# Moving a quarter of a modulation vector from one-column matmuls to VectorE: eight k-tiles added in two chains, then four one-column sums on PE

## The chip, the cores and the metric

One core of one Trainium2 chip. The metric is the device time of one execution in microseconds (us); lower is better. Before the change it is 831.41 us (median of 3 runs, 831.29 to 831.42).

PE is TensorE, PEld its weight loads, DVE is VectorE, ACT is ScalarE, SP issues the DMAs. All times inside a trace count from the start of its span.

## The reference, cut to what matters

```python
mod = (_silu(c) @ w_mod)            # six vectors of 1024: sa, ca, ga, sb, cb, gb
h = _layernorm(x) * (1 + ca) + sa   # x: 2048 x 1024
qkv = h @ wqkv                      # then linear attention, wo, and a SwiGLU FFN
```

Only the scale vector `ca` is touched, and of it only columns 768 to 1023. It is needed very early: the first q products multiply `h`.

## The kernel before

`h` is kept transposed in `HT`, so the scale is one value per partition for each k-tile `dt` (128 of the 1024 columns that the products sum over). The two vectors are made by one-column matmuls with the weights stationary, eight k-tiles per 128 columns, all in one corner of bank 0 of PSUM (where PE leaves its sums; the second index of the tile `PS` is the bank):

```python
def mod_sc(w, c0, ms):
    for m in ms:
        for kt in range(NDT):                       # NDT = 8
            P.pe("matmul", out=PS[:, 0, c0 + m:c0 + m + 1], lhsT=w[:, kt, m * 128:(m + 1) * 128],
                 rhs=SILUC[:, kt:kt + 1], start=mod_first[0], stop=(kt == NDT - 1), skip_group_check=True)
            mod_first[0] = False

def fin_ca(m, n):                                   # VectorE reads bank 0
    P.dve("tensor_scalar", out=MODCOL[:, 0, m:m + n], in0=PS[:, 0, 8 + m:8 + m + n], scalar1=1.0, ...)
```

The first q phase threads these between the q products (`q_part`, 512 columns wide, one bank per `nt`):

```python
# ... q products of k-tiles 0 and 1, scale columns 0 to 3 ...
mod_sc(WCA, 8, range(4, 8))            # 32 products
fin_ca(4, 4)
for dt in (4, 5):
    h0_scale_only(dt)                  # VectorE
for nt in range(7):
    q_part(nt, qb[nt], (2, 3))
act_stats(4)
for nt in range(7):
    if nt == 4:
        mod_sc(WSA, 0, range(6, 8))    # shift columns 6, 7: bank 0 again
        fin_sa(6, 2)
        for dt in (6, 7):
            h0_scale(dt)               # needs scale and shift columns 6, 7
    q_part(nt, qb[nt], (4, 5))
mod_sc(WSA, 0, range(4, 6))
fin_sa(4, 2, True)
for nt in range(7):
    if nt == 2:
        bias_mm((4, 5))                # one-column products, bank 0
    q_part(nt, qb[nt], (6,))
# ... k-tile 7, shift columns 0 to 3, then one long run of products ...
```

The helper that records the operations keeps, for each PSUM bank, the last operation of each engine, and makes an access wait for the other engines' last access of the whole bank, whatever the columns:

```python
for bank in banks:
    st = self.excl.get(bank)
    if st:
        for e2, d in st.items():
            if e2 != eng:
                deps_add(d)
    self.excl[bank] = {eng: op}
```

While the first chunk's q and k run on PE, the next chunk of `h` is transposed by DMA, four tiles one after the other, and then modulated (scaled and shifted) on VectorE, one k-tile at a time; the first k group of chunk 1 takes these k-tiles in order:

```python
def th_dma(st):
    xbar(HT[:, buf, :, j * 128:(j + 1) * 128], XRES[:, st, :])      # DMA transpose; st = 4 to 7 here
for dt in range(NDT):
    add(kside, 1, lambda dt=dt: th_mod(1, dt))                      # VectorE, 128 x 512 each
```

And at the start PE runs warm-up products on constant data: `warm(13, bank=3)`, later `warm(5, bank=3)`.

Of the kernel before, what the change touches and what calls it, by code (L numbers as in the profile page):

```python
# [6 lines left out]
BF16 = mybir.dt.bfloat16  # L7
U8 = mybir.dt.uint8
ACT = mybir.ActivationFunctionType
ALU = mybir.AluOpType  # L10
# [252 lines left out]
def bass_adaLN_cond__linear_attn_block__swiglu_ffn__prompt_kernel(  # L263
# [17 lines left out]
    NDT = D // 128  # L281
# [4 lines left out]
    with ExitStack() as es:  # L286
# [6 lines left out]
        def T(name, off, shape, dt):  # L293
            n = 1
            for s_ in shape[1:]:
                n *= s_
            assert off % 32 == 0 and off + n * mybir.dt.size(dt) <= ARENA, (name, off, shape)
            return nc.alloc_sbuf_tensor_at(name, shape, dt, offset=base + off)
# [4 lines left out]
        WCA = T("wca", 32 * KB, [128, NDT, D], BF16)  # L303
        WSA = T("wsa", 48 * KB, [128, NDT, D], BF16)
        AT = T("at", 72 * KB, [128, NFT, 512], BF16)
        SM = 64 * KB
# [7 lines left out]
        MODCOL = T("modcol", SM + 1120, [128, 4, NDT], FP32)  # L314
# [13 lines left out]
        ZCOL = T("zcol", SM + 2304, [128, NHG], FP32)  # L328
        RED = T("red", SM + 2336, [128, NDT], FP32)
        MASK4 = T("mask4", SM + 2368, [128, 4], BF16)  # L330
        BIASQ = T("biasq", SM + 2784, [128, NDT], FP32)
        SUMXH = T("sumxh", SM + 2816, [128, NST, 2], FP32)
        NMR = T("nmr", SM + 2944, [128, NST], FP32)
# [5 lines left out]
        HT = T("ht", 120 * KB, [128, 2, NDT, 512], BF16)  # L339
# [7 lines left out]
        ACC = T("acc", 192 * KB, [128, D], FP32)  # L347
        MHL = T("mhl", 196 * KB, [128, 2, D], BF16)
# [7 lines left out]
        SILUF = T("siluf", SM + 7744, [128, NDT], FP32)  # L356
# [22 lines left out]
        PS = nc.alloc_psum_tensor("ps", [128, 8, 512], FP32)  # L379
# [15 lines left out]
        P = _Prog()  # L395
# [47 lines left out]
        P.dve("memset", ap=MASK[:], constant=0.0)  # L443
        for h in range(4):
            P.dve("memset", ap=MASK[32 * h:32 * h + 32, 32 * h:32 * h + 32], constant=1.0)
        P.dve("memset", ap=MASK4[:], constant=0.0)
        for h in range(4):
            P.dve("memset", ap=MASK4[32 * h:32 * h + 32, h:h + 1], constant=1.0)
        P.dve("memset", ap=ZSEL[:], constant=0.0)
# [54 lines left out]
        def mod_sc(w, c0, ms):  # L504
            for m in ms:
                for kt in range(NDT):
# [4 lines that stand above are left out]
        def fin_ca(m, n):  # L511
            P.dve("tensor_scalar", out=MODCOL[:, 0, m:m + n], in0=PS[:, 0, 8 + m:8 + m + n], scalar1=1.0, scalar2=None,
                  op0=ALU.add)

        def fin_sa(m, n, cast=False):
            if cast:
                P.dve("tensor_copy", out=MODTMP[:, m:m + n], in_=PS[:, 0, m:m + n])
            P.dve("tensor_copy", out=MODCOL[:, 1, m:m + n], in_=PS[:, 0, m:m + n])

        def h0_scale_only(dt):  # L520
            P.dve("tensor_scalar", out=HT[:, 0, dt, :], in0=HT[:, 1, dt, :], scalar1=MODCOL[:, 0, dt:dt + 1],
                  scalar2=None, op0=ALU.mult)

        def h0_shift(dt):
            P.dve("tensor_scalar", out=HT[:, 0, dt, :], in0=HT[:, 0, dt, :], scalar1=MODCOL[:, 1, dt:dt + 1],
                  scalar2=None, op0=ALU.add)
# [7 lines left out]
        def bias_fin():  # L534
            P.dve("tensor_copy", out=BIASQ[:], in_=PS[:, 0, 16:24])

# [3 lines left out]
        def h0_first(dt, eng):  # L540
            if eng == "act":
                P.act("activation", out=HT[:, 0, dt, :], in_=t_view(dt), func=ACT.Copy, scale=MODCOL[:, 0, dt:dt + 1])
            else:
                P.dve("tensor_scalar", out=HT[:, 0, dt, :], in0=t_view(dt), scalar1=MODCOL[:, 0, dt:dt + 1],
                      scalar2=None, op0=ALU.mult)
# [8 lines left out]
        def h0_scale(dt):  # L554
            P.dve("tensor_scalar", out=HT[:, 0, dt, :], in0=HT[:, 1, dt, :], scalar1=MODCOL[:, 0, dt:dt + 1],
                  scalar2=MODCOL[:, 1, dt:dt + 1], op0=ALU.mult, op1=ALU.add)
# [17 lines left out]
        def act_stats(st, c0=0, mid=None):  # L574
            n = (D - c0) // 512
            junk0 = HT[:, 1, 0:2, :] if st < 8 else JUNK1
            for fn_, sc_, acc_ in ((ACT.Identity, 1.0 / D, SUMX), (ACT.Square, D ** -0.5, SUMSQ)):
                P.act("activation", out=junk0[:, 0:n, :], in_=XRES[:, st, c0:D].rearrange("p (a b) -> p a b", a=n),
                      func=fn_, scale=sc_, accum_out=acc_[:, st:st + 1])
                if mid is not None:  # L580
                    mid()
                    mid = None
# [90 lines left out]
        def q_part(nt, bank, dts):  # L673
            for dt in dts:
                P.pe("matmul", out=PS[:, bank, :], lhsT=WQK[:, dt, nt * 128:(nt + 1) * 128],
                     rhs=HT[:, 0, dt, :], start=(dt == 0), stop=(dt == 7))
# [56 lines left out]
        def q_phase_chunk0(side):  # L733
            qb = [1, 2, 3, 4, 6, 7, 5]
            for nt in range(4):
                q_part(nt, qb[nt], (0,))
            mod_sc(WCA, 8, range(2, 4))
            fin_ca(2, 2)
            for dt in (2, 3):
                h0_first(dt, "dve")  # L740
            for nts, dts in (((4, 5), (0,)), (range(6), (1,)), ((6,), (0, 1))):
                for nt in nts:
                    q_part(nt, qb[nt], dts)
            mod_sc(WCA, 8, range(4, 8))
            fin_ca(4, 4)
            for dt in (4, 5):
                h0_scale_only(dt)
            for nt in range(7):
                q_part(nt, qb[nt], (2, 3))
            act_stats(4)  # L750
            for nt in range(7):
                if nt == 4:
                    mod_sc(WSA, 0, range(6, 8))
                    fin_sa(6, 2)
                    for dt in (6, 7):
                        h0_scale(dt)
# [5 lines that stand above are left out]
                    bias_mm((4, 5))  # L762
                q_part(nt, qb[nt], (6,))
            for nt in range(7):
                if nt == 1:
                    mod_sc(WSA, 0, range(4))
                    fin_sa(0, 4, True)
                    ln_ops[1][0]()
                    ln_ops[1][1]()
                if nt == 4:  # L770
                    bias_mm(range(4))
                    bias_fin()
                q_part(nt, qb[nt], (7,))
            ln_ops[1][2]()
            ln1_rstd1(5)
            for f in act_mv_ops(4):
                f()
            neg_rstd(4)
            q_phi = lambda nt: phi_evac(qb[nt] if nt < 7 else 0, PQT[:, nt, 0:512], bias=BIASQ[:, nt:nt + 1])
            for i, dt in enumerate((4, 5, 0, 1, 2, 3, 6, 7)):  # L780
                P.pe("matmul", out=PS[:, 0, :], lhsT=WQK[:, dt, 896:1024], rhs=HT[:, 0, dt, :], start=(i == 0),
                     stop=(i == 7))
            for dt in (4, 5):
                h0_shift(dt)
            ln1_xn(5)
            th_dma(5)
            for dt in range(4):
                h0_shift(dt)
            ln1_xn(4)
            th_dma(4)  # L790
            for nt in range(8):
                q_phi(nt)
                for f in side.get(nt, []):
                    f()
            qk_ctr[0] = 0
# [40 lines left out]
        def z_cols():  # L836
# [4 lines left out]
                  in0=ZHL[:, 0, 0:NDT].unsqueeze(2).to_broadcast([128, NHG, 4]),  # L841
                  in1=MASK4[:].unsqueeze(1).to_broadcast([128, NHG, 4]), op=ALU.mult)

# [249 lines left out]
        for ch in range(NCH):  # L1093
            nxt = ch + 1 if ch + 1 < NCH else None
            for ft in range(NFT):
# [4 lines left out]
                for dt in range(NDT):  # L1100
                    P.pe("matmul", out=PS[:, gbank, :], lhsT=GUG[slot][:, dt, ftl * 128:(ftl + 1) * 128],
                         rhs=H2T[:, dt, :], start=(dt == 0), stop=(dt == NDT - 1))
                for dt in range(NDT):
                    P.pe("matmul", out=PS[:, ubank, :], lhsT=GUU[slot][:, dt, ftl * 128:(ftl + 1) * 128],
                         rhs=H2T[:, dt, :], start=(dt == 0), stop=(dt == NDT - 1))
# [4 lines left out]
                if ch == 0 and ft % 2 == 0 and ft < 14:  # L1110
                    i = ft // 2
# [11 lines left out]
                if nxt is None and ft in (8, 12):  # L1123
# [3 lines left out]
                          in1=GB_B[:, 896:1024].unsqueeze(1).to_broadcast([128, f1 - f0, 128]), op=ALU.mult)  # L1127
# [5 lines left out]
            for j in range(4):  # L1133
# [3 lines left out]
                if not last:  # L1137
                    for ft in range(NFT):
                        for nh in range(2):
                            P.pe("matmul", out=PS[:, bb + nh, :], lhsT=AT[:, ft, j * 128:(j + 1) * 128],  # L1140
                                 rhs=WD(ft)[:, nh * 512:nh * 512 + 512], start=(ft == 0), stop=(ft == NFT - 1))
                for nh in range(2):
                    i = nh
                    parts = [(0, 384, bb + 1), (384, 512, 4)] if last and nh == 1 else [(0, 512, bb + nh)]
                    for (c0, c1, pb) in parts:
                        if last:
                            for ft in range(NFT):
                                P.pe("matmul", out=PS[:, pb, c0:c1], lhsT=AT[:, ft, j * 128:(j + 1) * 128],
                                     rhs=WDG[:, ft, :] if c0 > 0 else WD(ft)[:, nh * 512 + c0:nh * 512 + c1],
                                     start=(ft == 0), stop=(ft == NFT - 1))  # L1150
# [46 lines left out]
```

## Time and profile before

| what | value | view |
|---|---|---|
| time, median | 831.41 us | runs |
| span in the profile | 829.3 us | page |
| PE busy | 99% | page |
| PE without a break | 12.29 to 827.1 us | chain in order of time |
| 16, 32 one-column products hold PE for | 0.40, 0.80 us | timeline of PE |

PE is the limit.

The end of the chain that ended last, in order of time (start, length, what):

```profile
12.29 814.80 PE ps L176 x4016
...
827.11 0.29 DVE xres L176
```

From 12.29 us on, for 814.80 us, nothing but PE is on it; only the last residual addition follows. A change after that is worth what it does to PE's own sequence.

The timeline of PE in the first q phase (start us, length us, engine, line, operation, out<-in, shape, count). The modelled end of a group of matmuls overlaps the next, so times are taken from start to start; a few matmul records are missing from some traces, as in a count of 21 for 22:

```profile
13.56 2.32 PE L176 MATMUL ps<-ht,wqk 128*128 128x512 bf16 x10
15.71 0.94 PE L176 MATMUL ps<-siluc,wca 128*128 128x1 bf16 x32
16.51 4.91 PE L176 MATMUL ps<-ht,wqk 128*128 128x512 bf16 x22
21.26 0.54 PE L176 MATMUL ps<-siluc,wsa 128*128 128x1 bf16 x16
21.66 1.46 PE L176 MATMUL ps<-ht,wqk 128*128 128x512 bf16 x6
...
27.84 1.46 PE L176 MATMUL ps<-ht,wqk 128*128 128x512 bf16 x6
```

32 scale products start at 15.71 and the next q product at 16.51: 25 ns each. 22 q products take 16.51 to 21.26: 0.216 us each. 16 shift products take 21.26 to 21.66. From the ten q products at 13.56 to the long run at 27.84 the stage takes 14.28 us. This interval leaves out when PE could start.

Two lines of VectorE's timeline in the same stretch, in brackets the idle time before them and what ended it. It has time to spare:

```profile
16.75 0.16 DVE L176 TENSOR_SCALAR modcol<-ps 128x4 f32<-128x4 f32 x1 [1.89 <-PE ps L176]
...
21.84 0.16 DVE L176 COPY modcol<-ps 128x2 f32<-128x2 f32 x1 [4.27 <-PE ps L176]
```

### The profile page before, as it was taken

The numbers are of one execution on the slowest core, as the hardware profiler recorded it, in microseconds if no ns is written. First come the engines' busy times: TensorE is split into PE (matmuls) and PEld (weight loads), VectorE is DVE, ScalarE is ACT, GpSimd is POOL, SyncE is SP. The second block draws the span as 40 slices with busy tenths as digits, with TensorE's granted clock in tenths as the row PEclk, the third lists the DMA queues.
The fourth block names the chain that finished last, engine by engine and source line by source line (L and its number), as shares of the span: only waits on it lengthen the run. The fifth ranks groups of instructions, "written<-read, shape, count | busy, mean of one in ns | idle before, by whom it ended". The sixth has DMA issues, their size and how long they took to land.

```text
span 829.3 us, 10017 instructions
## 1 busy us (share of the span) xinstructions
PE 823.3 (99%) x4083; PEld 378.8 (46%) x4083; DVE 312.9 (38%) x666; ACT 196.3 (24%) x335; POOL 40.5 (5%) x58
## 2 busy tenths in 40 slices
PE   8999999999999999999999999999999999999998
PEld 4544444454444444444444444444444444444444
DVE  5797986756955521121221111122111211221111
ACT  3658641323232111111111111111110111111011
POOL 1010000000130000030000003000000300000000
DMA  9969655938297986700455571045557004553000
GB/s 320 284 152 229 150 162 172 197 107 304 57 256 226 262 256 184 194 25 13 123 152 153 152 188 34 13 124 154 152 153 193 27 13 124 151 154 91 0 26 26
DMA packets 199246, 119.29 MB, mean 144 GB/s; under 512 B 57880, under 2 KB 182944, under 8 KB 199200
## 3 DMA queue, kind: packets, MB, share of 16 engines
q1 hardware_dynamic: 199184, 118.65, 53.0%
q8 instruction: 32, 0.52, 0.3%
q14 instruction: 14, 0.11, 0.0%
q10 hardware_dynamic: 16, 0.00, 0.0%
HBM read 100.67 MB, written 4.33 MB: 127 GB/s over the span
## 4 chain that ended last, share of the span: by engine, by line
PE 98%; DMA 1%; DVE 0%; ACT 0%; SPq 0%; POOL 0%; issue 0%
PE ps L176 98%; DMA xres<-in_A_x_dram 1%; ACT ht L176 0%; DVE xres L176 0%; SPq L176 0%; POOL rstd L176 0%; DVE stats L176 0%; DVE mv L176 0%; DVE ve L176 0%
## 5 line engine op out<-in xcount | busy, mean ns | idle before, releaser
L176 PE MATMUL ps<-h2t,gug 128*128 128x512 bf16 x896 | 211.7, 379 | 0.0
L176 PE MATMUL ps<-h2t,guu 128*128 128x512 bf16 x896 | 211.7, 379 | 0.0
L176 DVE TENSOR_TENSOR at<-sg,ps 128x512 bf16<-128x512 bf16 x112 | 77.0, 687 | 282.8 <-PE ps L176 281.2
L176 ACT ACTIVATE sg<-ps 128x512 bf16<-128x512 f32 x112 | 66.9, 597 | 309.7 <-PE ps L176 309.7
L176 PEld LDWEIGHTS ps<-h2t,guu 128*128 128x128 bf16 x896 | 87.7, 98 | 105.7
L176 PEld LDWEIGHTS ps<-h2t,gug 128*128 128x128 bf16 x896 | 87.6, 98 | 105.5
L176 PE MATMUL ps<-wd_a,at 128*128 128x512 bf16 (+1 forms) x512 | 112.4, 377 | 0.0
L176 PE MATMUL ps<-ht,wqk 128*128 128x512 bf16 x512 | 111.8, 379 | 0.1
L176 PE MATMUL ps<-wd_b,at 128*128 128x512 bf16 (+1 forms) x384 | 85.0, 377 | 0.0
L176 PEld LDWEIGHTS ps<-wd_a,at 128*128 128x128 bf16 x512 | 50.1, 98 | 59.7
L176 DVE TENSOR_TENSOR ut<-att,gb_b 128x512 bf16<-128x512 bf16 (+1 forms) x32 | 14.1, 441 | 167.0 <-ACT att L176 167.0
L176 PEld LDWEIGHTS ps<-ht,wqk 128*128 128x128 bf16 x512 | 49.4, 98 | 58.7 <-issue 0.2
L176 ACT ACTIVATE att<-ps 128x512 bf16<-128x512 f32 (+1 forms) x32 | 17.4, 591 | 182.1 <-PE ps L176 182.1
L176 PEld LDWEIGHTS ps<-wd_b,at 128*128 128x128 bf16 x384 | 37.6, 98 | 44.7
L176 PE MATMUL ps<-pk,xres 128*128 128x512 bf16 x256 | 56.5, 379 | 0.0
L176 PE MATMUL ps<-mw,pqt 128*128 128x512 bf16 x256 | 56.3, 379 | 0.0
L176 POOL TENSOR_SCALAR h2t<-h2t,modcol 128x512 bf16<-128x512 bf16 x32 | 26.3, 836 | 383.4 <-DMA h2t<-xn 383.4
L176 ACT ACTIVATE e<-ps 128x512 bf16<-128x512 f32 x56 | 33.1, 603 | 31.8 <-PE ps L176 21.3
L176 PEld LDWEIGHTS ps<-mw,pqt 128*128 128x128 bf16 x256 | 24.8, 98 | 30.2 <-DVE xres L176 0.4
L176 PEld LDWEIGHTS ps<-pk,xres 128*128 128x128 bf16 x256 | 24.8, 98 | 30.0 <-issue 0.4
L176 ACT ACTIVATE junk<-xres 128x1024 bf16<-128x1024 bf16 x24 | 25.4, 1058 | 35.1 <-DVE xres L176 34.9
L176 DVE SCALAR_TENSOR_TENSOR xres<-ps,xres 128x512 bf16<-128x512 f32 x32 | 21.4, 688 | 12.3 <-PE ps L176 11.5
(106 smaller groups left out, 345.1 us busy)
## 6 DMA issues: line engine op xcount, KB each, us to landing
gug<-in_B_w_gate_dram SPq DMA_DIRECT2D x56, 512.0 KB, 3.9
guu<-in_B_w_up_dram SPq DMA_DIRECT2D x56, 512.0 KB, 5.2
xres<-in_A_x_dram SPq DMA_DIRECT2D x20, 256.0 KB, 8.0
rb<-recip_den SPq DMA_DIRECT2D x8, 512.0 KB, 11.5
stgx<-in_w_mod_dram SPq DMA_DIRECT2D x2, 2048.0 KB, 7.8
wd_a<-in_B_w_down_dram SPq DMA_DIRECT2D x4, 1024.0 KB, 8.0
out_dram<-xres SPq DMA_DIRECT2D x31, 128.0 KB, 1.7
xres<-in_A_x_dram SPq DMA_DIRECT2D x3, 1024.0 KB, 14.2
```

The lines of the kernel that those rows point to most:

```text
L176: return getattr(e, method)(**kw)
```

## The change

The 16 products of scale columns 6 and 7 (768 to 1023) leave PE. VectorE multiplies and adds the eight k-tiles of these 256 columns in two alternating chains of fp32, adds the two, and splits the result into a bf16 part and a bf16 remainder. PE sums over the partitions: two 128-column pieces, times two parts, against a column of ones. The two scalings of k-tiles 4 and 5 go from VectorE to ACT, to make room. The intent is to free PE of 12 products net, with engines that idle.

```diff
+        P.dve("memset", ap=ONESC[:], constant=1.0)
...
+        def part_macc_ops(w, c0, n):
+            acc = [ACC[:, i * n:(i + 1) * n] for i in range(2)]
+            for kt in range(NDT):
+                a, src, sc = acc[kt % 2], w[:, kt, c0:c0 + n], SILUF[:, kt:kt + 1]
+                # ... kt < 2: tensor_scalar mult; else scalar_tensor_tensor mult, add into a
+            # ... acc[0] += acc[1]; MHL[0] = bf16(acc[0]); MHL[1] = acc[0] - MHL[0]
+        def part_sum(c0, ms):
+            for m in ms:
+                for i in range(2):
+                    P.pe("matmul", out=PS[:, 0, c0 + m:c0 + m + 1], lhsT=MHL[:, i, m * 128:(m + 1) * 128],
+                         rhs=ONESC[:], start=False, stop=(i == 1), skip_group_check=True)
...
         def h0_scale_only(dt):
-            P.dve("tensor_scalar", ...)
+            P.act("activation", ..., func=ACT.Copy, scale=MODCOL[:, 0, dt:dt + 1])
...
-            mod_sc(WCA, 8, range(4, 8))
-            fin_ca(4, 4)
+            mod_sc(WCA, 8, range(4, 6))
+            mops = part_macc_ops(WCA, 768, 256)
+            for f in mops[:4]:
+                f()
+            fin_ca(4, 2)
+            for f in mops[4:]:
+                f()
...
                 if nt == 4:
+                    part_sum(8, (6, 7))
+                    fin_ca(6, 2)
                     mod_sc(WSA, 0, range(6, 8))
```

(Cuts are marked with dots.)

More of the change, by code (lines that the diff above doesn't have):

```diff
@@ L330, in bass_adaLN_cond__linear_attn_block__swiglu_ffn__prompt_kernel @@
         MASK4 = T("mask4", SM + 2368, [128, 4], BF16)
+        ONESC = T("onesc", SM + 2400, [128, 1], BF16)
         BIASQ = T("biasq", SM + 2784, [128, NDT], FP32)
@@ L518, in fin_sa @@
             P.dve("tensor_copy", out=MODCOL[:, 1, m:m + n], in_=PS[:, 0, m:m + n])
+        def part_macc_ops(w, c0, n):
+            acc = [ACC[:, i * n:(i + 1) * n] for i in range(2)]
+            ops = []
+            for kt in range(NDT):
+                a, src, sc = acc[kt % 2], w[:, kt, c0:c0 + n], SILUF[:, kt:kt + 1]
+                if kt < 2:
+                    ops.append(lambda a=a, src=src, sc=sc: P.dve("tensor_scalar", out=a, in0=src, scalar1=sc,
+                                                                 scalar2=None, op0=ALU.mult))
+                else:
+                    ops.append(lambda a=a, src=src, sc=sc: P.dve("scalar_tensor_tensor", out=a, in0=src, scalar=sc,
+                                                                 in1=a, op0=ALU.mult, op1=ALU.add))
+            ops.append(lambda: P.dve("tensor_tensor", out=acc[0], in0=acc[0], in1=acc[1], op=ALU.add))
+            ops.append(lambda: P.dve("tensor_copy", out=MHL[:, 0, c0:c0 + n], in_=acc[0]))
+            ops.append(lambda: P.dve("tensor_tensor", out=MHL[:, 1, c0:c0 + n], in0=acc[0], in1=MHL[:, 0, c0:c0 + n],
+                                     op=ALU.subtract))
+            return ops
+        def part_sum(c0, ms):
[3 more added lines that the diff above has]
+                         rhs=ONESC[:], start=False, stop=(i == 1), skip_group_check=True)
         def h0_scale_only(dt):
-            P.dve("tensor_scalar", out=HT[:, 0, dt, :], in0=HT[:, 1, dt, :], scalar1=MODCOL[:, 0, dt:dt + 1],
-                  scalar2=None, op0=ALU.mult)
+            P.act("activation", out=HT[:, 0, dt, :], in_=HT[:, 1, dt, :], func=ACT.Copy,
+                  scale=MODCOL[:, 0, dt:dt + 1])
         def h0_shift(dt):
```

## The prediction

> **What bounds the kernel now.** TensorE. The page gives PE 99% busy; the chain that ended last, in order of time, is PE without a break from 12.29 us to 827.1 us, and the table of waits has no PE wait after that start. So the change is worth only what it takes from or adds to PE's own sequence between 12 and 28 us. DVE and ACT have room: in the timeline DVE idles from 14.9 to 16.75 and from 17.6 to 21.84, ACT from 14.8 to 25.9.
>
> **What leaves PE.** 16 of the 32 one-column products with the scale weights. In the timeline 16 such products hold back the next q matmul by 0.40 us (21.26 to 21.66), 32 by 0.80 (15.71 to 16.51): 25 ns each, as the Trainium skill states for small matmuls ("TensorE: Matmul & The Clock Gate", Back-to-back issue gap). Four new hi/lo products cost 0.10. Net -0.30 us.
>
> **What DVE gets.** Estimated from the trace's longer versions (128x1024: multiply-add 1279 ns, first multiply 750, copy 684, subtract 1226; multiply-add at 512 columns 688): at 256 columns two multiplies of 0.3 us, six multiply-adds of 0.4, add 0.4, copy 0.3, subtract 0.4: about 4 us. They start at about 14.9 (weights landed at about 13.95), let the read of columns 4-5 in at 16.4, and end at about 19.2; PE wants the sums at about 20.7. The two scalings moved to ACT (0.6 us each) end near 18; PE needs them at 19.2. None of this is critical.
>
> **What it adds as a wait.** The helper serializes whole PSUM banks between engines. The sum products write bank 0, VectorE then reads two columns of bank 0, and the next PE work is the shift products, also in bank 0. PE must wait for that read, with no q matmul between. The same handoff stands in the trace: after the products at 22.95, two q matmuls (0.43 us) precede the bias products, and these still start 0.10 us later than 22.95 + 0.40 + 0.43. VectorE does one read more there (0.07 us). So the bare handoff is 0.10 + 0.43 - 0.07 = about 0.46 us.
>
> **Sum.** -0.40 + 0.10 + 0.46 = +0.16 us; PE is saturated after it, so everything shifts by that. Predicted 831.6 us (from 831.41), 8 in 10 between 831.1 and 832.1. Faster by over 2%: 0.005; within 2%: 0.99; slower: 0.005. The PE time freed is 0.04% of the run, and the wait eats it.
>
> **What would show it.** In PE's timeline the scale products x32 at 15.7 become x16, and the q matmuls behind start about 0.40 us earlier (16.1). Near 20.8 stand four one-column products, then a new PE idle of 0.3 to 0.4 us, released by DVE writing the scale columns; the waits table gains this one entry. The long q run that starts at 27.84 starts at about 28.0. DVE's new group ends before 19.5, and PE never waits for it or for ACT's scalings.
>
> **What would make it wrong.** (a) The wait is shorter or hidden: -0.3 us at best. (b) The shift weights land only about 0.3 us before PE asks (8.07 + 12.7 = 20.8 against 21.05; 13.65 + 11.5 = 25.15 against 25.38), so an earlier PE would wait for DMA. (c) The DVE chain runs past 20.7 us: a PE stall of the overrun. (d) The start before 12.29 us, DMAs and LayerNorm, moves by some tenths and shifts everything.

## More of the kernel before

Lines of the page: span; busy time, share of the span and instructions of each engine; the DMA queue of kind "instruction" (packets, MB, share of 16 engines); the chain that ended last, by engine.

```profile
span 829.3 us, 10017 instructions
...
PE 823.3 (99%) x4083; PEld 378.8 (46%) x4083; DVE 312.9 (38%) x666; ACT 196.3 (24%) x335; POOL 40.5 (5%) x58
...
q8 instruction: 32, 0.52, 0.3%
...
PE 98%; DMA 1%; DVE 0%; ACT 0%; SPq 0%; POOL 0%; issue 0%
```

The line of q8 counts 32 packets with 0.52 MB together, 16 KB each, of a queue that the kernel never issues on.

Further on, the modulation of chunk 1 on VectorE, and PE's weight loads across the start of chunk 1:

```profile
42.62 2.67 DVE L176 TENSOR_SCALAR ht<-ht,modcol 128x512 bf16<-128x512 bf16 x8 [1.26 <-DMA ht<-xres]
```

```profile
41.01 6.14 PEld L176 LDWEIGHTS ps<-ht,wqk 128*128 128x128 bf16 x29
```

VectorE waited for the fourth transpose (`ht<-xres`) until 42.62. PE ran on without a wait.

## The result, and the profile after

After: 832.04 us median (831.93 to 832.7, 6 runs) against 831.41 (830.98 to 831.49, 6 runs) of before; ratio 1.001, 95% interval 0.9997 to 1.0023. A ratio here is the mean time of one kernel's fast runs over that of the other's of the same rounds, so it is not quite the ratio of the medians quoted. The stated range holds the time, with some luck: in a later call the same kernel's median was 832.22, outside it. The change itself does not come out as forecast: +0.63 us where +0.16 was said.

The page of after, the same four lines:

```profile
span 830.7 us, 9929 instructions
...
PE 819.3 (99%) x3993; PEld 378.5 (46%) x4071; DVE 316.7 (38%) x677; ACT 197.5 (24%) x337; POOL 40.6 (5%) x58
...
q8 instruction: 32, 0.52, 0.3%
...
PE 96%; DVE 1%; DMA 1%; issue 1%; SPq 0%; ACT 0%; DVEq 0%; ACTq 0%
```

The timeline of PE, first q phase:

```profile
13.67 2.32 PE L176 MATMUL ps<-ht,wqk 128*128 128x512 bf16 x10
15.82 0.54 PE L176 MATMUL ps<-siluc,wca 128*128 128x1 bf16 x16
16.58 4.92 PE L176 MATMUL ps<-ht,wqk 128*128 128x512 bf16 x21 [0.22 <-DMA wqk<-in_A_wqkv_dram]
21.34 0.24 PE L176 MATMUL ps<-onesc,mhl 128*128 128x1 bf16 x4
21.93 0.54 PE L176 MATMUL ps<-siluc,wsa 128*128 128x1 bf16 x16 [0.35 <-DVE modcol L176]
...
28.51 0.81 PE L176 MATMUL ps<-ht,wqk 128*128 128x512 bf16 x3
```

The scale products are 16 (15.82), the four sum products are there (21.34), and 0.35 us of idle (in brackets) before the shift products is released by VectorE's write of the scale columns, as predicted. But the q products behind the scale products start at 16.58, not at 15.82 + 0.40 = 16.22. The stage takes 28.51 - 13.67 = 14.84 us, 0.56 more than before. The table of PE's waits (us in total, times, longest) names the reasons; the first of its lines ended at 10.86, before the stage:

```profile
PE ps L176 <- DMA wca<-in_w_mod_dram: 0.9, 1, 0.9
...
PE ps L176 <- DVE modcol L176: 0.4, 1, 0.4
...
PE ps L176 <- DMA wqk<-in_A_wqkv_dram: 0.2, 1, 0.2
```

Weights landed late in this execution: PE waited for the q weights of k-tiles 2 and 3, and the freed time went into that wait.

VectorE's new group:

```profile
15.20 0.62 DVE L176 TENSOR_SCALAR acc<-wca,siluf 128x256 f32<-128x256 bf16 x2 [0.23 <-DMA wca<-in_w_mod_dram]
15.73 0.88 DVE L176 SCALAR_TENSOR_TENSOR acc<-wca,siluf,acc 128x256 f32<-128x256 bf16 x2
...
16.59 1.67 DVE L176 SCALAR_TENSOR_TENSOR acc<-wca,siluf,acc 128x256 f32<-128x256 bf16 x4
...
19.08 0.42 DVE L176 TENSOR_TENSOR mhl<-acc,mhl 128x256 bf16<-128x256 f32 x1
```

It ran from 15.20 to 19.50 (estimated 14.9 to 19.2), and PE did not wait for it.

That explains the first 28 us. It does not explain the rest: from the start of the long run to the end of the span, before took 829.34 - 27.84 = 801.5 us and after 830.72 - 28.51 = 802.2 us. The missing 0.7 us is at the start of chunk 1, where the change touches nothing. VectorE's modulation, and PE's weight loads:

```profile
44.13 2.03 DVE L176 TENSOR_SCALAR ht<-ht,modcol 128x512 bf16<-128x512 bf16 x6 [2.10 <-DMA ht<-xres]
```

```profile
41.02 3.34 PEld L176 LDWEIGHTS ps<-ht,wqk 128*128 128x128 bf16 x16
44.60 0.10 PEld L176 LDWEIGHTS ps<-ht,wqk 128*128 128x128 bf16 x1 [0.24 <-DVE ht L176]
44.92 0.10 PEld L176 LDWEIGHTS ps<-ht,wqk 128*128 128x128 bf16 x1 [0.23 <-DVE ht L176]
...
46.86 0.33 PEld L176 LDWEIGHTS ps<-ht,wqk 128*128 128x128 bf16 x3 [0.23 <-DVE ht L176]
```

VectorE began the modulation at 44.13, released by the fourth transpose, 2.10 us after it had nothing else to do (before: 42.62, after 1.26). PE caught up with it and waited eight times, for one k-tile after the other, at VectorE's pace of 0.32 us each (44.60 to 44.92) in place of PE's 0.216. In the profile of before there is no such wait. So the two profiled spans differ by 1.38 us: 0.11 in when the stage starts, 0.56 in the stage, 0.71 after it. (The profiled run of after took 832.48, above its median.)

### The profile page after: what moved, and what is told of

Same layout as the page of the kernel before. It is cut to its first block, busy times and chain, and to the rows that moved or that the text cites. A ratio compares the mean times of both kernels' runs of the same rounds, so it can differ in the third digit from the quotient of the medians.

```text
span 830.7 us, 9929 instructions
## 1 busy us (share of the span) xinstructions
PE 819.3 (99%) x3993; PEld 378.5 (46%) x4071; DVE 316.7 (38%) x677; ACT 197.5 (24%) x337; POOL 40.6 (5%) x58
## 4 chain that ended last, share of the span: by engine, by line
PE 96%; DVE 1%; DMA 1%; issue 1%; SPq 0%; ACT 0%; DVEq 0%; ACTq 0%
PE ps L176 96%; DMA wqk<-in_A_wqkv_dram 1%; DVE acc L176 1%; SPq L176 0%; DVE pkt L176 0%; DVE e L176 0%; DVE pqt L176 0%; ACT e L176 0%; DVE xres L176 0%; DVE ht L176 0%; DVE modcol L176 0%; DVEq L247 0%; ACTq L247 0%
## 6 DMA issues: line engine op xcount, KB each, us to landing
xres<-in_A_x_dram SPq DMA_DIRECT2D x3, 1024.0 KB, 14.1
```

## The experiments

The theory of the prediction was the handoff through bank 0. The first rival was lateness of the loads. After the first four runs a third theory was added, on the queue of 16 KB packets; the expectations call it the instruction-fetch theory. Each call of runs shares its runs of the kernel before.

### Both kernels again

> The kernel before, unchanged, against itself. It gives the noise of a ratio and a second profile. If the lateness of the loads in the profile of after (first scale weights landed at 10.8 us against 9.6 before, the last shift weights at 26.05 against 25.16) is luck of one execution, this second profile of before may show landings anywhere between 9.6 and 10.9 for the first scale weights. If the lateness belongs to the change, this profile shows 9.6 again. Ratio 1.000 either way.

r1_before: 831.58 us median (831.12 to 831.72) against 831.22 (830.83 to 832.09) of the same kernel. So two medians of one kernel differ by 0.36 us, and no difference of a few tenths can rest on medians alone; the intervals inside the traces have to carry it. The first scale weights landed at 10.47 us here, 9.62 in the first profile: lateness of loads is luck of the execution. The stage took 14.29 us, the rest 801.6.

> The kernel after, unchanged. Handoff theory: +0.16 us in any execution whose loads land as early as in the profile of before, and the new PE idle of 0.35 us before the shift products is there in every profile. Load theory: the time is +0.5 or more, and the profile shows PE waiting for loads (q weights near 16.5 us, shift weights near 26) as in the first profile of after.

r2_after: 831.67 us (831.19 to 831.82) against 831.22. This profile had early loads (first scale weights at 9.25 us), and shows the handoff alone:

```profile
13.18 2.32 PE L176 MATMUL ps<-ht,wqk 128*128 128x512 bf16 x10
15.34 0.54 PE L176 MATMUL ps<-siluc,wca 128*128 128x1 bf16 x16
15.74 4.91 PE L176 MATMUL ps<-ht,wqk 128*128 128x512 bf16 x21
20.48 0.24 PE L176 MATMUL ps<-onesc,mhl 128*128 128x1 bf16 x4
21.08 0.54 PE L176 MATMUL ps<-siluc,wsa 128*128 128x1 bf16 x16 [0.35 <-DVE modcol L176]
...
27.66 1.67 PE L176 MATMUL ps<-ht,wqk 128*128 128x512 bf16 x7
```

The stage takes 27.66 - 13.18 = 14.48 us, 0.20 more than before (14.28); 0.16 was predicted. Four products take 20.48 to 20.58, and PE goes on at 21.08: the handoff is 0.50 us, predicted 0.46. And still the rest of the span took 802.2 us, with eight waits of PE's weight loads for the modulation, as in the first profile of after. Neither theory had said that.

### e1_sum_early: take the handoff away

```diff
-                if nt == 4:
+                if nt == 2:
                     part_sum(8, (6, 7))
                     fin_ca(6, 2)
+                if nt == 4:
                     mod_sc(WSA, 0, range(6, 8))
```

> The four sum products and the read of their columns two k-groups earlier, so that four q matmuls (0.86 us) stand between the read and the shift products. Handoff theory: the PE idle of 0.35 us before the shift products is gone and the run is 0.4 us shorter than after, 0.25 to 0.3 below before. Load theory (PE waits for the shift weights anyway): the wait goes over to the DMA of the shift weights, and the run is at most 0.15 us shorter than after.

831.35 us (830.9 to 832.33) against 831.22. The profile fell on the slowest run:

```profile
19.74 0.24 PE L176 MATMUL ps<-onesc,mhl 128*128 128x1 bf16 x4
19.85 1.02 PE L176 MATMUL ps<-ht,wqk 128*128 128x512 bf16 x4
21.55 0.55 PE L176 MATMUL ps<-siluc,wsa 128*128 128x1 bf16 x16 [0.68 <-DMA wsa<-in_w_mod_dram]
```

The wait for VectorE is gone, but PE, now early, waited 0.68 us for the shift weights, whose last piece landed at 21.51. Without that the q products end at about 20.72 and the stage would have taken about 14.1. In this execution the load theory won; the handoff's removal is right in kind and can be collected only when the loads allow (e6 below collects it: a stage of 13.98 us, 0.30 below before). What was late is one piece: 15 of the 16 landing records of these shift weights had come by 19.54. The straggler shows first in the q weights before them (15 pieces by 16.64, the last at 18.56), which were in flight while the first 16 KB packet passed (16.34 to 17.44). So this wait may well be a collision of the same kind as the one below; no run tests it. The rest took 802.4 us.

### e2_handoff_in_before: the handoff alone

```diff
-            mod_sc(WCA, 8, range(4, 8))
-            fin_ca(4, 4)
+            mod_sc(WCA, 8, range(4, 6))
+            fin_ca(4, 2)
...
                 if nt == 4:
+                    mod_sc(WCA, 8, range(6, 8))
+                    fin_ca(6, 2)
                     mod_sc(WSA, 0, range(6, 8))
```

> The kernel before with the 16 products of scale columns 6 and 7 moved, unchanged, to just before the shift products, and their read by VectorE made a second read there: the handoff alone, without the VectorE chain, the freed PE time or the scalings on ACT. Handoff theory: before +0.46 us, PE idle of 0.35 us before the shift products released by DVE. Load theory: before within 0.15 us, except for what an execution's loads add.

831.47 us (831.18 to 831.6) against 831.22. The stage took 14.83 us, 0.55 more than before, nothing else being changed:

```profile
20.43 0.54 PE L176 MATMUL ps<-siluc,wca 128*128 128x1 bf16 x16
21.38 0.54 PE L176 MATMUL ps<-siluc,wsa 128*128 128x1 bf16 x16 [0.41 <-DVE modcol L176]
```

16 products from 20.43 to 20.83, then 0.55 us until the next. (The shift weights' last piece landed at 21.23, so a part of this may be theirs.) The rest took 801.5 us, with two waits for the modulation. So the extra 0.7 us late in the run does not come from the handoff. It stood in after, r2_after and e1, which have 12 PE products less, and not in before, r1_before and e2.

### The third theory

The trace's DMA records hold the 32 packets of 16 KB one by one. The third of them stood at 39.25 to 40.22 us in before and at 41.99 to 42.97 in after. It comes when PE has begun 332 to 334 weight loads, in both. After executes 12 one-column products less before that point, so it gets there about 12 q products later: 12 x 0.216 = 2.6 us; 2.7 us were seen. A transpose leaves 16 landing records, called its pieces here; the page counts 16 DMA engines, and one piece for each is assumed. Of the fourth transpose, in before all land from 42.35 to 42.50; in after 15 land by 42.39 and the last at 44.01.

The Trainium skill says of this ("Runtime: NRT & Kernel Launch", Instruction fetch mechanics) that an engine's instructions are refilled in 16 KiB blocks of 256 by a DMA queue of its own, and calls the cost of a block boundary "mostly hidden". The block size fits: 256 instructions are 128 pairs of load and matmul, and in before the next such packet came 126 loads later; from the 16th packet on they come 124 to 129 loads apart; PE's 8166 instructions fill 32 blocks. The early packets do not keep to a count, though: the first came at 97 to 130 loads over all 14 profiles, the second at 270 to 289, and in after the fourth came 135 loads behind the third. The same skill ("DMA: Bandwidth & Descriptors", Queues, rings and completion order) says that a DMA engine serves its queues in turn, packet by packet. From this it is inferred, not stated there, that a 1 us packet on one engine can hold back that engine's piece of whatever else is in flight. The records do not name the engine; the next runs test the position of the fetch instead.

### e3_after_plus12: put the instructions back, behind the sums

```diff
                     part_sum(8, (6, 7))
+                    for _ in range(12):
+                        P.pe("matmul", out=PS[:, 0, 24:25], lhsT=MHL[:, 0, 768:896], rhs=ONESC[:], start=False, ...)
```

> After, with 12 useless one-column products behind the four sum products, so that PE has executed as many instructions by 30 us as in the kernel before. Instruction-fetch theory: the 16 KB fetch that stood at 41.1 to 42.0 us in the profiles of after stands at 39 to 40 us, the last of the 16 pieces of the fourth transpose of h lands within 0.2 us of the others (it was 1.5 to 1.6 us late), VectorE starts the modulation of chunk 1 at 42.4 to 43.0 us, and the span is 829.4 to 829.7 us, 0.3 us or more below after although PE has 0.3 us more to do. Handoff and load theories: after plus 0.3 us.

831.79 us (831.26 to 831.8) against 831.15. Half a hit. The fetch stood at 39.94, all pieces of the fourth transpose landed from 43.12 to 43.25, PE never waited for the modulation, and the rest took 801.5 us: the 0.7 us is gone. But the time, 0.64 us above before, is no better than after's in two of three (0.63, 0.45 and, later, 1.02): the stage took 15.0 us, with the 0.3 us of useless products inside, the handoff, and late q weights (last piece 16.32). The modulation started at 43.37, later than the 43.0 expected.

### e4_before_minus12 and e9_before_minus12_again: the fetch moved in the kernel before

```diff
-            mod_sc(WCA, 8, range(4, 8))
+            mod_sc(WCA, 8, range(4, 6))
+            for m in (6, 7):
+                for kt in range(2):      # two of eight k-tiles: wrong on purpose
+                    P.pe("matmul", out=PS[:, 0, 8 + m:9 + m], lhsT=WCA[:, kt, m * 128:(m + 1) * 128], ...)
```

> Before, with only two of the eight k-tiles in the products of scale columns 6 and 7: 12 PE products less, nothing else (no VectorE chain, no handoff, no work on ACT); the result is wrong on purpose. Instruction-fetch theory: the fetch moves from 39 to about 41.5 us, the fourth transpose has a piece that lands about 1.6 us late, the modulation of chunk 1 starts at 43.2 to 44.1 us, and the kernel is 0.3 to 0.6 us SLOWER than before though PE has 0.3 us less to do. Any other theory: 0.3 us faster, at worst equal.

> Before with 12 products fewer, a second profile. The first profile (830.46 us, its fastest run) had the fetch at 40.5 us and no late piece; the other runs took 831.0 to 831.8. Instruction-fetch theory: a profile of a run near 831.5 shows the fetch near 41 us and a late piece of the fourth transpose; one near 830.5 shows none. Other theories: 0.3 us below before throughout.

e4: 831.46 us (830.46 to 831.78) against 831.15. e9: 831.42 (830.72 to 833.32) against 831.20. With 0.3 us less to do on PE (the stage of e4 took 13.98 us) the medians are 0.2 to 0.3 us above before, not 0.3 below; the ratios are 1.0002 (0.9989 to 1.0014) and 0.9999 (0.9986 to 1.0013). A gain of 0.3 us would be a ratio of 0.9996, inside both intervals, so the times settle nothing and the profiles have to. (The comparison with the reference passed all the same; its tolerance does not see the missing products.)

The profile of e4 fell on its fastest run. There the fetch began at 40.54 and lasted 1.83 us, no piece of the fourth transpose was late (40.89 to 41.05), and the rest took 801.5 us. This is against the expectation. It is not that the fetch was elsewhere: it began 0.35 us before the first piece landed, in the five profiles with a late piece 0.26 to 0.31 us before. Here the fetch took long (1.83 us) and the transpose did not; what decides between the two is not shown. Nor is this span, 0.62 us below before's, a gain from the rest: 0.30 of it is the stage and 0.31 an earlier start. The profile of e9 fell on its slowest run, one with a slow start (granted clock 0.998). There the fetch stood at 42.73, the last piece landed at 44.83 with 15 landed by 43.19, and the table of waits has

```profile
PEld ps L176 <- DVE ht L176: 1.8, 8, 0.2
```

which is eight waits with 1.8 us in total, the mark of after, in a kernel without any of the change's VectorE or ACT work. That no profile of a run near 831.5 was had leaves a gap: that those runs had the collision is inferred.

### e5_sum_early_plus12, e8_sum_early_plus12_again: both costs taken away

```diff
         warm(5, bank=3)
+        for _ in range(12):
+            P.pe("matmul", out=PS[:, 3, 0:1], lhsT=IDENT[:], rhs=E1[:, 0, 0:1], start=True, stop=True)
```

(on top of e1)

> The early-sum version with 12 useless one-column products at about 9 us, where PE idles. Instruction-fetch theory: the fetch at 41.85 us goes back to 39 to 40 us, no late piece of the fourth transpose, span 829.0 to 829.5 us, at or below before; but the first fetch (16.3 us) comes up to 2.6 us earlier as well and may delay the q weights of k-tiles 2 and 3 on one engine (PE wait for them near 16 us of up to 0.6 us). Otherwise equal to the early-sum version.

> The early-sum version with the 12 early products, again: the candidate for the best version. Both effects gone: 0.2 to 0.5 us below before in the median, 0.3 us below the version with the handoff in the same call.

e5: 830.71 us (830.59 to 831.36) against 831.15, ratio 0.9997 (0.9985 to 1.001). e8: 831.06 (830.63 to 831.47) against 831.20, ratio 0.9998 (0.9986 to 1.0011). The fetch stood at 39.78 and 39.68, no late piece in either, rest 801.6 and 801.5 us. The stages took 14.45 and 14.29 us, with PE waiting for the shift weights in e5 and for the q weights in e8, so the gain of PE time was again spent on loads. One thing was expected and did not come: the first fetch did not move with the 12 early products (16.52 and 16.53 us, 16.50 in before). Both medians are below before, 0.44 and 0.14 us (for e8 0.2 to 0.5 was expected), and e8 is 0.19 below e7, which keeps the handoff (0.3 expected); the intervals include no change. It is the fastest version measured, and is not shown to beat before.

### e6_sum_early_fetch_later: move the fetch past the transpose

```diff
-        warm(13, bank=3)
+        warm(10, bank=3)
...
-        warm(5, bank=3)
+        warm(0, bank=3)
```

(on top of e1)

> The early-sum version with 8 warm-up products fewer (5 of the second group, 3 of the first), which puts every later fetch about 1.7 us later instead of earlier. Instruction-fetch theory: the fetch stands at 42.8 to 43.7 us, after the fourth transpose has landed, so no late piece, the modulation of chunk 1 starts at 41.6 to 42.5 us, and the span is 828.9 to 829.4 us, below before. If warm-up products matter, the first transposes and q products run at a slower clock and the gain goes. Otherwise equal to the early-sum version.

832.56 us (831.89 to 833.76) against 831.15, ratio 1.0019 (1.0005 to 1.0033): slower by an interval that excludes no change, in the way that the expectation named for it. The fetch went to 46.05 (42.8 to 43.7 expected) and the transposes were free of it: issue of the fourth to the start of the modulation took 3.27 us, the least of all. But without the eight warm-up products the ten q products started at 15.07 us, 1.5 later than in before: the first four q products took 1.42 us, to the scale products at 14.67, against 0.86 in before, and the mean granted clock was 0.998. With PE this late no load was waited for in the stage, and it took 13.98 us: the -0.30 us that is left when the handoff is gone. The fetch theory stands; the version is no use.

### r5_after_again and e7_after_plus12_early: the fetch alone

> The kernel after, a third profile, beside the two versions that follow. Instruction-fetch theory: again the 16 KB fetch at 41 to 42 us, again one of the 16 pieces of the fourth transpose 1.5 us late. If the pieces land together in this profile, the collision is not a property of the change.

> After, with 12 useless one-column products at about 9 us, where PE idles anyway, so that nothing but the position of the instruction fetches changes. Instruction-fetch theory: fetch at 39 to 40 us, the pieces of the fourth transpose within 0.2 us, 0.3 to 0.6 us faster than after in the same call; the handoff of 0.5 us stays. Other theories: equal to after.

e7 is after with the 12 useless products of e5 at about 9 us, and nothing else. r5: 832.22 us (831.86 to 834.08), ratio 1.0015 (1.0003 to 1.0028). e7: 831.25 (831.11 to 832.02), ratio 1.0003. Before: 831.20. Twelve useless instructions make after 0.97 us faster in the median; the slowest run of e7 is inside the range of r5, the other four are all below it. Not all of this is the fetch: in the profiles 0.60 us is in the rest and 0.41 in the stage, where r5 waited for the q weights (e7's own profile, of its slowest run, loses 0.80 by a later start). r5's profile again has the fetch at 41.78, the late piece (43.84, the others by 42.19) and eight waits. e7's has the fetch at 40.04, no late piece, and this at the start of chunk 1 (PE's weight loads):

```profile
45.83 0.10 PEld L176 LDWEIGHTS ps<-ht,wqk 128*128 128x128 bf16 x1 [0.16 <-DVE ht L176]
46.15 0.10 PEld L176 LDWEIGHTS ps<-ht,wqk 128*128 128x128 bf16 x1 [0.23 <-DVE ht L176]
46.47 0.76 PEld L176 LDWEIGHTS ps<-ht,wqk 128*128 128x128 bf16 x5 [0.23 <-DVE ht L176]
```

Three short waits in place of eight, and a rest of 801.5 us (r5: 802.1). The table of waits has first r5, then e7:

```profile
PEld ps L176 <- DVE ht L176: 1.8, 8, 0.2
PEld ps L176 <- DVE ht L176: 0.6, 3, 0.2
```

The handoff stayed (stage 14.48 us, as in r2).

### All 14 profiles side by side

Read from the DMA records, the landing records and the timelines. "Fetch" is the third 16 KB packet; "loads" the PE weight loads begun by then; "transpose" the landing of the first, the 15th and the last piece of the fourth transpose; D the time from the issue of that transpose to the start of the modulation; "waits" those of PE's weight loads for it; "stage" and "rest" as above.

```
run         fetch        loads transpose            D     waits  stage  rest
before      39.25-40.22  334   42.35 42.49 42.50   4.18   0     14.28  801.5
r1_before   38.82-39.84  332   42.67 42.80 42.81   4.03   3     14.29  801.6
e2          39.66-40.62  336   42.66 42.81 42.81   4.34   2     14.83  801.5
e3          39.94-40.85  334   43.12 43.24 43.25   4.19   0     15.00  801.5
e7          40.04-41.33  334   43.49 43.62 43.62   4.41   3     14.48  801.5
e5          39.78-40.70  336   42.85 42.97 42.98   4.47   3     14.45  801.6
e8          39.68-40.60  335   42.80 42.92 42.93   4.36   2     14.29  801.5
after       41.99-42.97  332   42.25 42.39 44.01   5.03   8     14.84  802.2
r2_after    41.10-42.09  332   41.41 41.55 43.18   5.05   8     14.48  802.2
r5_after    41.78-42.66  332   42.05 42.19 43.84   5.01   8     14.89  802.1
e1          41.85-42.77  333   42.13 42.32 43.88   5.20   8     14.90  802.4
e9          42.73-43.79  332   43.03 43.19 44.83   5.02   8     14.50  802.2
e4          40.54-42.37  331   40.89 41.01 41.05   3.33   0     13.98  801.5
e6          46.05-47.01  340   42.67 42.79 42.80   3.27   1     13.98  801.8
```

Three groups stand out by D. With the fetch at 39 to 40 us it is 4.0 to 4.5 us; the fetch overlaps the third transpose. With the fetch at 41 to 43 us it is 5.0 to 5.2, with one late piece. In e6, with the fetch out of the way, and in e4, where it delayed no piece, 3.3. The rest of the span takes 801.5 to 801.6 us in the first group and 802.1 to 802.4 in the second; in the third it is 801.5 (e4) and 801.8 (e6; why not 801.5 was not followed up). So 801.5 looks like PE's own work, and a still earlier modulation has nothing more to give.

## Why the prediction was right or wrong

- **PE is the limit, 16 products free 0.40 us, four cost 0.10.** Right: 15.34 to 15.74 in r2_after for 16. The Trainium skill ("TensorE: Matmul & The Clock Gate", Back-to-back issue gap) states about 25 ns for small matmuls. The runs agree: 16 one-column products with their weight loads take 0.40 us.
- **VectorE's chain of about 4 us, 1.5 us to spare, PE never waits for it or for ACT.** Right: 15.20 to 19.50 us, and no such wait.
- **A bare handoff of 0.46 us.** Right in kind and nearly in size: 0.50 us in r2_after. The term -0.40 + 0.10 + 0.46 came out as +0.20 us where the loads were early.
- **An earlier PE would wait for loads.** Named as a risk for the shift weights, and seen for them in e1; for the q weights, which it did not name, in after and r5_after. In these executions the freed 0.4 us was not there to take; stages of 14.84 and 14.89 us.
- **"PE is saturated after it, so everything shifts by that."** This is the step that failed. The sum lacked a term: +0.6 to 0.7 us at the start of chunk 1 (rest 802.1 to 802.2 us in three profiles of after, 801.5 and 801.6 in two of before). The 12 removed PE instructions moved PE's own instruction fetch, by 2 to 3 us, from the third to the fourth transpose of the next chunk of `h`. One of the 16 pieces of the transpose landed 1.6 us late, the modulation began late, and PE ran its next eight products at VectorE's pace. The prediction took PE's unbroken run to mean that everything PE consumes later has slack. In fact the modulation had almost none: in r1_before PE already waited for it three times.

How far it is shown: that the position of the fetch decides is shown by e7 against r5, where 12 useless products are the only difference, by e3, where they stand at another place and do the same, and by the split of 14 profiles into groups. Three things stay open. That the late piece sits on the DMA engine that carries the fetch is inferred from the times, and loads of the next `x` tiles were in flight there too. In e4 a fetch at nearly the same place delayed nothing. And the first fetch stayed at 16.2 to 17.3 us in 13 of 14 profiles whether or not the 12 products stood before it, so PE's count of products does not set every fetch. The total is less certain than its parts: after stood 0.63, 0.45 and 1.02 us above before, 0.2 of handoff plus 0.65 of collision plus up to 0.4 of waits for loads, more or less by the luck of the start.

## What to carry to other kernels

Removing instructions from a saturated engine was not only less work here: it shifted when that engine fetched a block of its instructions, and in a stage with little slack that one packet of about 1 us cost 0.6 to 0.7 us. When a change of a few tenths of a microsecond does not add up, compare the two traces interval by interval to the end, not only where the change is, and compare several profiles of each. Before freeing 0.3 us on an engine, look at what else in that stage is just in time (weights, transposes, a bank read by another engine): the freed time is worth only their slack.

## What the Trainium skill lacked or had wrong

- "Runtime: NRT & Kernel Launch", Instruction fetch mechanics, calls the cost of a block boundary "mostly hidden". Here one of the 32 refills (the fetches above), the third, took 0.9 to 1.3 us in 13 of 14 profiles (1.83 in e4), and where it met the fourth transpose it came with one piece 1.6 us late and cost the kernel 0.6 to 0.7 us (five of six such profiles). That a refill competes with the kernel's own transfers is not said there; "DMA: Bandwidth & Descriptors" lists refill among the runtime's own queue rows and has the sharing of engines by queues, but gives no cost of the one to the other.
- The same section gives the block of 256 instructions, but not what follows from it for tuning: with 12 products less in front of it the third refill came at 40.5 to 42.7 us in place of 38.8 to 40.0, at 331 to 336 weight loads in 13 of 14 profiles (46.0 us and 340 in e6). The first refill did not follow such a count (97 to 130 loads); what sets it is not shown.
